# A new instruction order, engine choice and buffer slots for a fused adaLN attention and gMLP kernel

## The chip, the cores and the metric

The kernel runs on one core of one Trainium2 chip. The metric is device time in microseconds of one execution, as the median of several runs; smaller is better. The core has five instruction queues that run side by side and wait for each other by semaphores: PE (TensorE, matrix products), ACT (ScalarE), DVE (VectorE), POOL (GpSimd) and SP, which here only issues DMAs.

## The reference

Two blocks on x of 2048 rows and 448 columns in bf16, each behind a layernorm with a scale and a shift that come from a condition vector c:

```python
mod = (_silu(c) @ w_mod).reshape(1, 6, 1, -1)          # sa, ca, ga, sb, cb, gb
h = _layernorm(x) * (1 + ca) + sa
x = x + ga * _A_ref(h, A_wqkv, A_wo)                   # 16 heads of 28, causal, window of 256 keys
h = _layernorm(x) * (1 + cb) + sb
x = x + gb * _B_ref(h, B_w_in, B_w_sp, B_b_sp, B_w_out)
# _B_ref:
z = _gelu(x @ w_in); z1 = z[..., :896]; z2 = _layernorm(z[..., 896:])
g = w_sp @ z2 + b_sp[:, None]                          # mixes the 2048 positions
return (z1 * g) @ w_out
```

## The kernel before

All data stay in SBUF. The 2048 rows are 16 tiles of 128 (j or t below) or 4 blocks of 512 (tb). The program first makes a list of 1236 numbered operations, each with the engines that it may run on, its dependencies, and the buffers that it takes from pools of slots. The order in which they are issued, on all engines at once, is a string of words, `ORDER`. A word is number, engine (p, a, v, g, s for PE, ACT, DVE, POOL, SP) and the slot of each buffer taken:

```python
for word in ORDER.split():
    n, eng, *slots = word.split(".")
    op, e = self.ops[int(n)], ENGS["pavgs".index(eng)]
    ...
    for h, k in zip(op.take, slots):
        h.slot = h.res.options[int(k)]
    ...
    self.prog[e].append(op)
```

Each engine's program is the words of that engine in their order. Waits on semaphores are then worked out from dependencies and slots (an operation that takes a slot waits for all users of its former owner), so every order is a correct program as long as it doesn't deadlock. Durations in the list (`dur`) no longer decide anything. 42 warming products of the list stand in neither string.

The stages, with the lines that the profile shows and the numbers of operations that matter here:

- *Start.* SP loads x (0, 1 the first two halves of 224 KB; 14, 17, 18 the rest), parts of w_mod (3, 4, 5), and the weights of q (6, 7, 8), k (9, 10, 11) and v (12, 13). Line 561 are products that only keep PE busy. Line 596/597 pads the q and k weights (130 to 137), lines 605 to 627 normalise x, line 692 transposes on PE, line 699/701 scales the result into hT (163 to 173), line 740 is the first q and k product (174 on), line 767/768 evicts it.
- *Attention, for j from 0 to 15, two halves each.* Line 952 is the wide score block (434 is the first of this kind, 819 the last), line 961 a further block of scores; line 913 on ACT is the exponential: one of 128 x 2048 (PW, 1.88 us) and one of 128 x 512 for each half, 128 x 1024 for the first two j (383 is the first). Line 968 on DVE masks, line 995 on PE multiplies with V, lines 1009 and 1011 divide into one of three o_sb slots. A DMA transpose on SP puts that into hT (line 477, hT<-o_sb), line 1019 multiplies with wo (801 for j = 14, 830 for j = 15), line 1024 adds to x, lines 605 to 633 normalise again, a second DMA transpose (hT<-xn) follows, and line 1044 scales it on ACT, DVE or POOL. Products of later blocks (line 782 q and k, 824 v, 811 the last k) are strewn between these, with the evictions of lines 792, 816 and 828. The four wide score banks are one buffer, so each wide score block waits for the exponential before it.
- *gMLP in.* Line 1081 makes z (gelu 1092/1104 on ACT; normalised by lines 605 to 617 and 1096/1099, or by 1108 to 1118), line 1127 makes z1 (gelu 1135).
- *Mixing.* 28 groups (line 1151) of 16 products of 128 x 512: each needs all 16 tiles of z and all 16 slices of one half of w_sp, wspA (863 + 1 + slice: operations 864 to 879) for tb 0 and 1, or wspB (880 to 895) for tb 2 and 3. These slices are DMA transposes of SP too. wspA lies where the attention's q buffers were: six of its slices may be loaded before the attention ends, the others and all of wspB not. Line 1155 on DVE adds the bias (bsp_bc, loaded by 863 with one plain DMA of 512 KB), line 1158 on POOL multiplies with z1.
- *Out.* Line 1170 multiplies with w_out, seven products for a tile, line 1181 on DVE adds x, line 1186 stores. The last tile is cut into three column pieces (1224/1225, 1228/1229, 1232/1233 on PE; 1226, 1230, 1234 on DVE; 1227, 1231, 1235 on SP).

## Time and profile before

| | |
|---|---|
| median of 3 runs | 274.05 us (273.52 to 274.32) |
| span of the profiled execution, first to last instruction | 271.3 us |
| PE busy | 262.8 us, 97% of the span |
| DVE, ACT, POOL busy | 154.9, 137.9, 105.6 us |
| PE weight loads busy (beside PE) | 142.2 us |
| HBM read and written | 9.53 and 1.84 MB |

The time of the profiled execution itself is not recorded beside its span; the runs' median is 2.75 us above the span. "Busy" counts an engine while at least one of its instructions runs; instructions that only wait, branch or issue a DMA don't count. A name such as `ps<-wspA,z` is output<-inputs; PEld is PE's loading of weights, which runs beside its products; SPq is SP's issuing.

### The profile page before, as it was taken

To read this page: it belongs to the slowest core of one execution; us is meant where nothing else is said; L and a number is where in the kernel's file an instruction comes from. 1 tells how busy PE (TensorE), PEld (TensorE's weight loads), DVE (VectorE), ACT (ScalarE), POOL (GpSimd) and SP (SyncE) were. 2 spreads that over 40 slices of the span, in tenths; PEclk is the share of its full clock that TensorE was granted. 3 is DMA by queue.
4 is the path that set the end of the run, shared out by engine and by line. 5 is a ranking of instruction groups with operands and counts; after the bars stand their busy time and mean duration, and the time that the engine had idled before them with its cause. 6 is when DMAs were issued, how large, how long until landed. Compare 5 with 4: busy or idle time off the path is not lost.

```text
span 271.3 us, 7454 instructions
## 1 busy us (share of the span) xinstructions
PE 262.8 (97%) x3207; PEld 142.2 (52%) x3231; DVE 154.9 (57%) x380; ACT 137.9 (51%) x190; POOL 105.6 (39%) x161
## 2 busy tenths in 40 slices
PE   6899999999999999999999999999999999999995
PEld 3665565666578665444544444444444444444543
DVE  6789996999999999998382001131102230136623
ACT  3699999999999997799996400000000000000000
POOL 8740528101244533671558401565003631155220
PEclk9999999999999999999999999999999999999999
DMA  7959846442137678557999999600000000001212
GB/s 212 305 195 339 140 109 90 81 61 41 21 65 128 86 98 158 106 111 105 162 205 175 184 211 167 78 0 0 0 2 0 0 0 2 0 0 49 86 53 85
DMA packets 67594, 26.53 MB, mean 98 GB/s; under 512 B 58021, under 2 KB 66474, under 8 KB 67562
## 3 DMA queue, kind: packets, MB, share of 16 engines
q1 hardware_dynamic: 67288, 25.61, 47.8%
q8 instruction: 25, 0.41, 0.7%
q10 hardware_dynamic: 274, 0.46, 0.4%
q14 instruction: 7, 0.06, 0.1%
HBM read 9.53 MB, written 1.84 MB: 42 GB/s over the span
## 4 chain that ended last, share of the span: by engine, by line
PE 84%; ACT 9%; DVE 2%; DMA 2%; issue 2%; SPq 1%; DVEq 0%
PE ps L1151 35%; PE ps L1081 8%; PE ps L1127 8%; PE ps L1170 8%; PE ps L782 5%; ACT PW L913 5%; PE ps L995 5%; PE ps L952 4%; PE ps L1019 4%; PE ps L824 3%; PE ps L961 2%; DMA wq_st<-in_A_wqkv_dram 2%; DVE hT L728 1%; PE ps L811 1%; ACT qT L767 1%
## 5 line engine op out<-in xcount | busy, mean ns | idle before, releaser
L913 ACT ACTIVATE PW<-ps 128x2048 bf16<-128x2048 f32 (+1 forms) x56 | 67.9, 1255 | 1.8 <-PE ps L952 0.7
L1155 DVE TENSOR_TENSOR tmpg<-ps,bsp_bc 128x512 bf16<-128x512 f32 x28 | 19.0, 689 | 85.6 <-PE ps L1151 74.0
L1158 POOL TENSOR_TENSOR z1T<-tmpg,z1T 128x512 bf16<-128x512 bf16 x28 | 31.9, 1152 | 75.3 <-DVE tmpg L1155 75.3
L1151 PE MATMUL ps<-wspB,z 128*128 128x512 bf16 x218 | 48.8, 379 | 0.3
L1151 PE MATMUL ps<-wspA,z 128*128 128x512 bf16 x219 | 48.6, 379 | 0.4 <-POOL z L1096 0.2
L968 DVE TENSOR_TENSOR PT<-PW,mask 128x1024 bf16<-128x1024 bf16 x56 | 36.7, 683 | 0.7 <-ACT PW L913 0.7
L1151 PEld LDWEIGHTS ps<-wspA,z 128*128 128x128 bf16 x224 | 21.9, 98 | 26.7 <-POOL z L1096 0.5
L1151 PEld LDWEIGHTS ps<-wspB,z 128*128 128x128 bf16 x224 | 21.9, 98 | 26.3
L613 POOL TENSOR_TENSOR rs_all<-ve_all,neghalf 128x1 f32<-128x1 f32 (+1 forms) x31 | 20.6, 674 | 33.7 <-DVE ve_all L610 32.4
L995 PE MATMUL ps<-Vaug,PT 128*128 128x32 bf16 x496 | 23.9, 177 | 0.0
L995 PEld LDWEIGHTS ps<-Vaug,PT 128*128 128x128 bf16 x496 | 21.9, 96 | 3.8 <-DVE o_sb L1011 0.6
L1170 PE MATMUL ps<-w_out_g,z1T 128*128 128x448 bf16 (+2 forms) x126 | 21.9, 332 | 0.0
L1081 PE MATMUL ps<-w_in,hT 64*128 64x448 bf16 x224 | 21.9, 349 | 0.0
L1127 PE MATMUL ps<-hT,w_in 64*128 64x512 bf16 x196 | 21.8, 376 | 0.0
L995 PE MATMUL ps<-Vaug,PW 128*128 128x32 bf16 x224 | 20.1, 176 | 0.0
L605 DVE BATCH_NORM_STATS2 st_all<-x_sb 128x6 f32<-128x448 bf16 x32 | 19.0, 611 | 0.0
L995 PEld LDWEIGHTS ps<-Vaug,PW 128*128 128x128 bf16 x224 | 17.6, 96 | 2.2
L782 PE MATMUL ps<-hT,WQK 128*128 128x512 bf16 x67 | 17.3, 379 | 1.3 <-DVE PT L988 0.2
L1170 PEld LDWEIGHTS ps<-w_out_g,z1T 128*128 128x128 bf16 x126 | 11.7, 98 | 10.0
L1135 ACT ACTIVATE z1T<-ps 128x512 bf16<-128x512 f32 x28 | 14.3, 609 | 4.2 <-PE ps L1127 4.2
L1081 PEld LDWEIGHTS ps<-w_in,hT 64*128 64x128 bf16 x224 | 10.7, 94 | 10.6 <-ACT PW L913 0.4
L952 PE MATMUL ps<-qT,KT 32*128 32x64 bf16 (+2 forms) x1008 | 15.3, 198 | 0.3 <-ACT PW L913 0.2
(122 smaller groups left out, 339.6 us busy)
## 6 DMA issues: line engine op xcount, KB each, us to landing
out_dram<-fin SPq DMA_DIRECT2D x15, 112.0 KB, 1.7
x_sb<-in_A_x_dram SPq DMA_DIRECT2D x3, 448.0 KB, 5.3
wmod<-in_w_mod_dram SPq DMA_DIRECT2D x1, 1344.0 KB, 9.5
w_in<-in_B_w_in_dram SPq DMA_DIRECT2D x1, 1344.0 KB, 9.1
QBD<-qT SPq DMA_DIRECT2D x16, 64.0 KB, 2.4
w_out_g<-in_B_w_out_dram SPq DMA_DIRECT2D x1, 784.0 KB, 6.6
bsp_bc<-in_B_b_sp_dram SPq DMA_DIRECT2D x1, 512.0 KB, 5.9
x_sb<-in_A_x_dram SPq DMA_DIRECT2D x2, 224.0 KB, 3.5
```

The costliest lines, as they stand in the source:

```text
L605: st = [dve(0.62 if True else 0, lambda e, t=t, ci=ci, s=s: e.bn_stats(st_all[:, slot, t, ci, :], s()), deps(t), prio) for ci, s in enumer ...
L613: rs = pool(0.41 + 0.155 * len(tiles), lambda e: e.tensor_tensor(rs_all[:, slot, a:b], ve_all[:, slot, a:b], neghalf[:, 0:b - a], ALU.pow) ...
L782: m = pe(4 * MMS, [lambda e, h=h, g=g, kc=kc, tb=tb: e.matmul(ps[:, h.slot[0], :], lhsT=WQK[:, kc, 4 * g:4 * g + 4, :].rearrange("p a b -> ...
L913: ex = act(xdur, lambda e, out_ap=out_ap, in_ap=in_ap: e.activation(out_ap(), in_ap(), ACT.Exp, scale=SCALE), [s], v - 8.0 + u, takes, tab ...
L952: fm.append(lambda e, hm=hm, k=k, qi=qi, key=key, kn=kn, lo=lo, hi=hi, col=col, p0=p0, t=t, j=j: e.matmul(ps[p0:p0 + kn, hm.slot[t], k * 1 ...
L968: return dve(0.68, lambda e: e.tensor_tensor(cols(hp.slot[0] * 2048 + 1024 * k, [[256, 4], [128, 2], [1, 128]]), cols(at_w() + 128 + 192 * ...
L995: fns.append(lambda e, hp=hp, hO=hO, hi=hi, bi=bi, kb=kb, hd=hd, nb=nb, a=at[hi][bi], p_of=p_of: e.matmul(ps[:, hO.slot[0], 32 * hd:32 * h ...
L1081: return lambda e, kc, p0, start, stop: e.matmul(ps[:, hs[t % 2].slot[hf], 0:D], lhsT=hT[p0:p0 + 64, kc, t * 128:(t + 1) * 128], rhs=w_in[ ...
L1127: return lambda e, kc, p0, start, stop: e.matmul(ps[:, hs[b // 2].slot[b % 2], :], lhsT=w_in[p0:p0 + 64, kc, ft * 128:(ft + 1) * 128], rhs ...
L1151: m = pe(16 * MMS, [lambda e, h=h, si=si, ft=ft, tb=tb: e.matmul(ps[:, h.slot[0], :], lhsT=z2[:, si, ft * 128:(ft + 1) * 128], rhs=(wspA i ...
L1158: u = pool(1.16, lambda e, ht=ht, ft=ft, tb=tb: e.tensor_tensor(z1T[tb][:, ft, :], tmpg[:, ht.slot[0], :], z1T[tb][:, ft, :], ALU.mult), [ ...
L1170: return [lambda e, ft=ft: e.matmul(ps[:, h.slot[0], c0:c1], lhsT=z1T[t // 4][:, ft, (t % 4) * 128:(t % 4 + 1) * 128], rhs=w_out_g[:, ft, ...
```

## The change

Only the string `ORDER` is replaced. It comes from a newly written search that uses distances measured in the trace of the kernel before. The same 1194 numbered operations are issued. Their order on every engine is new; 108 of the operations that may go to two or three engines change engine (37 from DVE to POOL, 30 from POOL to DVE, 20 from ACT to DVE, 17 from DVE to ACT, 2 each way between ACT and POOL); and most buffer slots are others. The lines that matter here, from both strings:

```diff
-2.a 25.v 35.g 0.s 26.v 27.v 28.v 38.g 39.g 3.a 4.s 36.g 45.a 33.g 29.v 5.s 30.v 31.v 37.g 32.v 40.g 6.s 7.s 41.g 46.p.0 48.a 47.a 144.v 8.s 145.v 1.s
...
-266.a 434.p.0 285.v 252.a 117.s 269.p.1 282.v 279.v 435.a.4.0 115.s 286.v 419.v 387.p 391.p 280.v 393.p 284.v 263.p.0 227.v 287.v 336.v 270.a 288.g
...
-985.p.1 808.v.0 923.g 809.v 943.a 901.v 986.p 810.s 987.p 944.v 903.v 988.a 937.v 966.p.0 873.s 924.v 945.a.0 967.p.3 936.v 955.v 968.p 995.a 874.s
...
-845.g 1110.p.6 1059.a 883.s 840.g 1058.a 1057.a 1088.a 893.s 1089.a 1056.a 1140.p.7 894.s 886.s 887.s 1107.p.0 891.s 863.s 892.s 1104.p.1 884.s 895.s
-1134.p.2 889.s 885.s 1131.p.3 1135.v.0 1105.v.1 1136.g 1098.p.4 1132.v.0 1133.g 844.g 1106.g 1095.p.5 1137.p.2 1096.v.0 1108.v.1 1097.g 841.g 1141.v.0
...
-1212.p.1 1187.s 1222.v.3 1223.s 1213.p 1224.p.4 1214.v.2 1225.p 1228.p.2 1229.p 1232.p.3 1226.v.0 1215.s 1233.p 1227.s 1234.v.1 1235.s 1230.v.3 1231.s
+0.s 3.a 35.g 25.v 28.v 36.g 38.g 2.a 4.s 37.g 33.g 61.p.3 26.v 5.s 34.g 65.p.5 42.g 1.s 72.p.5 57.p.1 43.g 7.s 45.a 58.p.5 39.g 138.v 8.s 46.p.1
...
+245.p.1 250.v 219.s 385.p.0 416.a 387.p 246.v 220.s 113.p.0 247.v 23.s 227.a 434.p.0 282.v 390.v 114.a 280.v 251.p.1 285.v 435.a.0.0 115.s 283.v 118.s
...
+856.v 932.p.1 833.v 779.v.0 834.g 857.v 1043.a 835.g 933.p 780.v 855.v 781.s 858.a 902.v 836.g 934.p 808.g.2 935.a 955.v 984.p.0 903.v 809.g 904.v
+1042.a 954.v 837.g.1 810.s 985.p.3 943.a 838.g 986.p 905.g 839.s 966.p.2 988.a 967.p.1 989.v 868.s 987.p 956.v 990.v 968.p 995.a 870.s 969.p 860.g
...
+863.s 1030.a 873.s 963.g 1003.p 999.g 1004.p 844.g 1005.a 1076.p.2 945.a.0 846.g 1006.v 1077.p.0 1025.v 869.s 1013.a 1078.p 1026.v 946.v 1007.v
...
+1086.p 977.g 887.s 1087.p 842.g 1095.p.4 1091.a 895.s 1088.a 1089.a 1059.a 893.s 1090.a 1058.a 884.s 1104.p.0 883.s 882.s 1107.p.1 880.s 890.s 889.s
+1134.p.2 888.s 894.s 1098.p.3 1135.v.0 886.s 1136.g 1125.p.2 1099.v.0 1206.p.3 1137.p.5 1207.v.1 1208.g 840.g 1108.v.1 1109.g 1158.p.6 1161.p.1
...
+1179.p.0 1183.v.1 1184.s 1188.p.1 1180.v.0 1181.s 1224.p.0 1189.v.2 1225.p 1228.p.2 1190.s 1226.v.3 1229.p 1232.p.1 1230.v.1 1227.s 1233.p 1231.s
+1234.v.0 1235.s
```

The order of SP behind the attention, in words: before, wspA slices 864 and 865 were issued among the hT transposes, then the other 14 of wspA, 11 of wspB, the bias load 863, and 5 of wspB. After, 872, 865, 866 and 876 are issued among the hT transposes; behind the last of these come 6 of wspA, the bias load, 3 of wspA, 2 of wspB, 3 of wspA, and 14 of wspB. The mixing groups ran in the order tb 0, 1, 0, 0, 1, 1, 0, 0, 1, 1, 2 (1170), 2, 3 and so on; now they run tb 0, 0, 0, 1, 0, 1, 3 (1206), 1, 2 and on.

More of the change, by code (lines that the diff above doesn't have):

```diff
@@ new lines @@
+594.p 646.a.3.4 540.p.0 400.v 513.v 401.v 456.v 639.p.0 595.v 514.v 355.p.1 613.v 515.g 428.g 402.g 596.v.0 640.a 666.p.0 429.g 541.v 614.p.0
+667.a.4.1 620.v 618.p.0 615.p 359.p.0 457.v 621.v 458.g 430.g 622.p 459.v 619.a 360.v 460.g.0 674.p.0 356.v 647.p.0 675.a.1.2 431.g.1 623.p 353.p.0
+624.v 403.g 461.v 432.v 516.g 625.v.1 462.s 326.p.1 354.v 648.a 678.v 695.p.0 327.a 597.s 357.p.0 641.v 696.a.2.3 642.v 668.p.0 626.s 643.p.0 671.v
+365.p.1 679.v 358.a 124.s 669.a 703.p.0 649.v 366.a 121.s 644.p 699.v 676.p.0 704.a.5.0 367.p.0 361.s 650.v 362.s 569.p.1 670.v 364.s 651.p 404.g.2
```

92 lines of the change are left out of this document (43 added, 49 removed).

## The prediction

> **What bounds the kernel now.** I read the page first (busy shares, then the chain of waits), then the windows by stage, and then the single places that the change touches. The page:
>
> ```profile
> span 271.3 us, 7454 instructions
> PE 262.8 (97%) x3207; PEld 142.2 (52%) x3231; DVE 154.9 (57%) x380; ACT 137.9 (51%) x190; POOL 105.6 (39%) x161
> ...
> PE 84%; ACT 9%; DVE 2%; DMA 2%; issue 2%; SPq 1%; DVEq 0%
> ```
>
> PE is busy for 262.8 of 271.3 us and makes up 84% of the chain. The windows (start:end, length, then the busy time of each engine) show where the missing 8.5 us are:
>
> ```profile
> 0.00:10.00 10.00, 7.37 (x67) 3.93 (x68) 6.99 (x25) 4.60 (x9) 7.04 (x20) 1.00 0.85 248
> 10.00:30.00 20.00, 18.92 (x268) 12.04 (x269) 17.95 (x56) 18.53 (x32) 8.24 (x14) 1.00 0.87 263
> 30.00:105.00 75.00, 73.87 (x1854) 49.15 (x1863) 69.94 (x153) 73.25 (x77) 27.78 (x42) 1.00 0.50 77
> 105.00:150.00 45.00, 45.00 (x464) 21.57 (x458) 31.60 (x103) 38.48 (x69) 25.45 (x54) 1.00 0.84 153
> 150.00:260.00 110.00, 109.25 (x510) 50.63 (x518) 23.79 (x37) 3.04 (x6) 35.97 (x33) 1.00 0.27 49
> ```
>
> PE idles 2.63 us before 10 us (it has nothing landed), 1.08 us from 10 to 30, 1.13 us in the attention (30 to 105), nothing from 105 to 150, and 0.75 us from 150 to 260; the rest is the end. In the attention ACT (73.25 of 75) and DVE (69.94 of 75) are almost as full as PE. The change leaves every matmul in place, so a better order can win only these idle times. What lies between 10 and 260 us is 1.08 + 1.13 + 0.75 = 2.96 us; with the end (below) some 3.3 us is the most that can be had. Nothing limits a loss in that way. Durations below are of this profiled execution, whose span is 271.3 us; the median of the runs, 274.05 us, is 2.75 us longer, and I carry that difference over unchanged. Differences under 0.3% (0.82 us) are about what a measurement of this kernel can't tell from none.
>
> **The start.** In the new order SP issues the second x half (1) ahead of the q weights (7, 8, 6), and on DVE and ACT the operations of the first tiles are dealt out anew.
>
> ```profile
> 3.05 4.63 DMA wq_st<-in_A_wqkv_dram
> 8.68 2.98 PE L740 MATMUL ps<-hT,WQK 128*128 128x256 bf16 x23 [0.43 <-DVE hT L701]
> ...
> x_sb<-in_A_x_dram SPq DMA_DIRECT2D x2, 224.0 KB, 3.5
> wq_st<-in_A_wqkv_dram SPq DMA_DIRECT2D x2, 224.0 KB, 4.5
> ```
>
> The q weights land at 3.05 + 4.63 = 7.68 us and the first product runs at 8.68. With 224 KB of x ahead of them instead of 112 KB of weights they land some 0.45 us later (half of 224 KB at the 248 GB/s of the first window). But before, the DVE did one of the weight paddings and then two hT evictions one after the other; now ACT evicts the first hT chunk while DVE pads. That gives 0.4 us back. I take 0 for the first product, with ends of +0.5 and -0.4.
>
> **The attention.** From the list of the new order: fewer products stand ahead of the first wide score block (434). Gone from before it are 265 and 251, four products of line 782 each.
>
> ```profile
> 46.03 1.76 PE ps L782 x8
> ...
> 26.35 1.88 ACT L913 ACTIVATE PW<-ps 128x2048 bf16<-128x2048 f32 x1
> ...
> 102.24 3.01 ACT L913 ACTIVATE PW<-ps 128x512 bf16<-128x512 f32 x3
> ...
> L913 ACT ACTIVATE PW<-ps 128x2048 bf16<-128x2048 f32 x28 | 53.0, 1894 | 1.5 <-PE ps L952 0.7
> L913 ACT ACTIVATE PW<-ps 128x512 bf16<-128x512 f32 x28 | 17.3, 617 | 0.3
> ```
>
> Eight products are 1.76 us, so PE reaches that block about 1.7 us of work sooner. Whether the attention also ends sooner is ACT's matter: from the first wide exponential at 26.35 to the end of the last at 105.25 ACT works through 28 wide ones of 1.89 us, with smaller operations of about 0.6 us between them. I counted these between the first and the last wide one: 51 before, 49 after, thus 1.2 us less of ACT work. On the other hand six operations that stood behind the first score exponential now stand ahead of the first wide one (19 from 383 to 435 against 13). So the first wide one starts only 0 to 1 us sooner, and the last ends between 0 and 2 us sooner if nothing else waits. In the attention alone PE can give 1.13 us. I take an attention that ends 0.3 us sooner, near the lower end, because PE, ACT and DVE are all over 93% busy there.
>
> **The weights of the mixing stage: what is late next.** After the attention SP has one row of transposing loads to issue, and PE starts the mixing stage (line 1151) when all 16 slices of wspA have landed and all z are ready.
>
> ```profile
> 118.58 6.34 SPq L477 DMA_TRANSPOSE hT<-xn  x4
> 124.96 19.74 SPq L477 DMA_TRANSPOSE wspA<-in_B_w_sp_dram  x14
> 144.74 15.89 SPq L477 DMA_TRANSPOSE wspB<-in_B_w_sp_dram  x11
> 160.68 0.58 SPq L1056 DMA_DIRECT2D bsp_bc<-in_B_b_sp_dram  x1
> 161.30 9.35 SPq L477 DMA_TRANSPOSE wspB<-in_B_w_sp_dram  x5
> ...
> 150.33 1.62 PEld L1151 LDWEIGHTS ps<-wspA,z 128*128 128x128 bf16 x9 [0.49 <-POOL z L1096]
> ...
> 150.56 10.74 PE ps L1151 x49
> 161.35 10.74 PE ps L1151 x49
> ...
> L1096 POOL TENSOR_SCALAR z<-z,rs_all,ve_all 128x896 bf16<-128x896 bf16 x4 | 4.3, 1087 | 0.7 <-DVE ve_all L617 0.7
> ...
> DMA to landing us min/median/max: 3.0/4.0/5.0
> ...
> DMA to landing us min/median/max: 3.5/4.1/6.4
> ```
>
> (The two landing lines are those of wspA and of wspB.) A transpose takes 19.74 / 14 = 1.41 us of the queue. The 5 behind the bias load take 9.35, so that load costs 0.6 + 9.35 - 5 x 1.41 = 2.9 us of queue. The new order issues four wspA slices early, where the old one issued two, and moves the bias load (863) from behind 11 wspB slices to behind 6 wspA slices. The last wspA slice is again the 14th of the final row, now with the bias ahead of it: it is issued at 124.96 + 13 x 1.41 + 2.9 = 146.2 and lands 3.0 to 5.0 later, at 149.2 to 151.2, 150.2 by the median. Before, the stage started at 150.33, 0.49 us late for a z on POOL; in the old order four such z of 1.09 us stood in one block at POOL's end, in the new one two of them come earlier, so the last z is up to 2.2 us sooner. So the transfers take the place of the z wait: a start at 150.2, unless the row of transposes starts earlier too. Even a faster PE before it would wait here.
>
> The new order also runs a group on wspB (1206) as the seventh, where the first was the eleventh. One group is 16 products; the pieces of the chain step by 10.79 us for 50 (49 recorded), so 3.45 us each, and the seventh starts at 150.3 + 20.7 = 171.0. The last wspB slice was issued at 161.30 + 9.35 - 1.41 = 169.2; with two fewer in the row it goes at 166.4 and lands 3.5 to 6.4 later, 170.5 by the median. The wait for it is 0 by the median, at most 1.8 us. I take 0.1. The other transfers that were moved (the x and w_in loads in the attention) land many microseconds ahead of use.
>
> **The end.** Of the last tile's three column pieces DVE now evicts 1230 before 1234, in the order in which PE makes them; before, it waited for the last piece first.
>
> ```profile
> 268.19 1.38 SPq L1186 DMA_DIRECT2D out_dram<-fin  x3
> 268.46 0.46 DVE L1181 TENSOR_TENSOR fin<-ps,x_sb 128x112 bf16<-128x112 f32 x2 [0.30 <-PE ps L1170]
> ...
> 236.84 1.32 PE ps L1170 x7
> ...
> L1181 DVE TENSOR_TENSOR fin<-ps,x_sb 128x448 bf16<-128x448 f32 (+2 forms) x18 | 10.0, 570 | 9.0 <-PE ps L1170 8.3 <-DMA out_dram<-fin 0.6
> ```
>
> Both small evictions came after PE's end (0.46 us), and the last of three issues ended at 268.19 + 1.38 = 269.57. With one eviction and one issue under PE's last products, one issue fewer stands at the end: 1.38 / 3 = 0.46 at most, 0.37 taken. The other late groups use three PSUM banks in turn, but one eviction (0.57 us) fits under each 1.32 us of products, so I cost that at nothing; if that cover fails, it is some 0.6 us once.
>
> **Sum of the forecast:** start 0, attention -0.3 (which reaches the end only as far as the transfers let it: -0.1), wait for wspB +0.1, end -0.4: span 270.9, time **273.7 us**. Its own range is 273.2 to 274.9, mostly within 0.3%.
>
> **Rivals.**
>
> *The lead goes through (faster).* If ACT turns its shorter row and the earlier first block into an attention that ends 1.2 us sooner, the last hT transposes (118.58 to 124.92) and the row behind them move too, and with the end 0.4 us that is 274.05 - 1.6 = **272.4 us**. For it: 1.2 us less of ACT work and less idle PE from 10 to 30. Against: the last hT are now scaled on POOL (808, 809, 837, 838), one after the other.
>
> *The bias load pushes the weights (slower).* If it blocks the queue as badly as at 161.30 or worse and a landing takes the maximum, wspA lands at 151.2 and wspB at 172.8 against a need at 171.0: PE loses 1.8 us in all. From a landing after 171.0 on each microsecond counts in full. 274.05 - 0.4 + 1.8 = **275.5 us**.
>
> *POOL and DVE get in each other's way in the attention (slower).* The change moves more operations to POOL (39 to it, 30 off it), among them hT and xn scalings.
>
> ```profile
> L1044 POOL TENSOR_SCALAR hT<-hT,modT x2: 767/1200/1632, 91.8 to 101.0; 128x512 bf16<-128x512 bf16 x2
> ```
>
> The same scaling on POOL took 767 ns once and 1632 ns once. Twelve of these long ones are new on POOL and ten are gone. If three of the twelve stretch by 0.87 us and hold up DVE and with it PE, that is 2.6 us: 274.05 - 0.4 + 2.6 = **276.3 us**. Against: DVE's work in the attention stays the same, and POOL is under 40% busy there. [...]
>
> That the new order does nothing but its better end (273.7) is in the forecast.
>
> **How the numbers follow.** Forecast 0.35; the lead goes through 0.31; the bias load 0.2; POOL and DVE 0.1; something slower that I don't see (a buffer slot that is wanted again too early, o_sb among them, whose slots no longer go round in turn) 0.04. Faster by over 0.3% (under 273.23) is the second case and a little of the forecast: 0.33. Slower by over 0.3% (over 274.87) is the last three: 0.34 with a little of the forecast put in: 0.35. Within: 0.32. For 8 in 10 the range goes from 271.9 (the lead and 0.5 us at the start) to 276.4 (the POOL case).
>
> **What would show it.** Right: the first load of weights of line 1151 waits for a DMA and not for POOL, at about 150; the seventh group starts near 171; the last issue to out_dram ends near 269.0 in an otherwise equal span; idle PE from 30 to 105 stays near 1.1 us. The lead: the last wide exponential ends before 104.3 and wspA's row from before 124. The bias: a gap of PE of over 0.5 us at the seventh group. POOL: line 1044 or 684 on POOL with a mean over 1.2 us. The prediction would be wrong if PE idles much more than 1.1 us in the attention or if PE's busy time itself changes.

## The result: slower by 2.5%, and the time is lost ahead of the mixing stage

| | before | after |
|---|---|---|
| median of the runs beside each other | 274.19 us (273.52 to 274.82) | 280.74 us (280.25 to 281.16) |
| ratio, 95% interval | | 1.0251 (1.0223 to 1.0278) |
| profiled execution: time, span | span 271.3 us | 280.85 us, span 278.9 us |

The forecast was 273.7 us, the range up to 276.4. In a second comparison the same new order took 281.21 us, 1.0295 of before (1.0264 to 1.0325): its times spread more than those of before (280.25 to 283.59), for a reason that the profiles below show. A ratio leaves out executions that took over 1.5% more than the fastest of the same kernel (two of six in e1, one of five in e9, two of six in e14, one of six in e15, four of seven in e17; their mean clock was 0.988 or 0.994), while a median counts every execution.

The two profiled spans are 7.6 us apart, the medians 6.55. The profiled execution of before was one of its shortest: later executions of it with the same span of 271.3 us took 273.0 to 273.1 us, about 1 us less than the median of 274.05 that the prediction set beside this span.

All lines of the profile of after stand one higher than before (L952 is L953). The page of after: 3.0 us more of busy PE (part of it products at half clock in the first 12 us, below), and a chain of waits of which PE makes up 70%, before 84%:

```profile
span 278.9 us, 7451 instructions
PE 265.8 (95%) x3209; PEld 142.3 (51%) x3231; DVE 158.3 (57%) x376; ACT 137.3 (49%) x187; POOL 111.5 (40%) x168
...
PE 70%; DVE 12%; issue 6%; POOL 5%; ACT 3%; DMA 3%; DVEq 0%; POOLq 0%
```

The same windows as in the prediction (PE's busy time is the third number): 7.04, 18.52, 71.52 and 43.70 against 7.37, 18.92, 73.87 and 45.00. PE idles 3.5 us in the attention, where before it idled 1.13, and 1.3 us from 105 to 150, where it idled not at all.

```profile
0.00:10.00 10.00, 7.04 (x56) 3.51 (x57) 6.12 (x22) 4.47 (x8) 5.61 (x18) 1.00 0.85 244
10.00:30.00 20.00, 18.52 (x250) 12.27 (x250) 18.69 (x52) 17.51 (x30) 6.56 (x11) 1.00 0.49 153
30.00:105.00 75.00, 71.52 (x1786) 46.30 (x1789) 69.36 (x153) 70.16 (x74) 30.88 (x44) 1.00 0.56 102
105.00:150.00 45.00, 43.70 (x500) 21.48 (x500) 30.75 (x91) 36.81 (x62) 28.02 (x56) 1.00 0.87 150
```

PE's waits in after (line, what it waited for, us in total, times, longest) show new places. Three are waits for c (line 519), for hT of block 2 (line 783), and "issue", which is no wait for any engine. The first row is a wait for a DVE copy: it names line 618, the last DVE instruction to end, but the product reads WQK, which DVE's copy 137 had been writing until just before (rows below).

```profile
PE ps L741 <- DVE ve_all L618: 1.2, 1, 1.2
PE ps L519 <- DMA c_row<-in_c_dram: 1.1, 1, 1.1
PE ps L783 <- DVE mv_all L609: 1.1, 2, 0.9
PE ps L953 <- issue: 0.8, 1, 0.8
...
PE ps L1152 <- POOL z L1097: 0.7, 1, 0.7
...
PE ps L1020 <- DMA hT<-o_sb: 0.4, 1, 0.4
```

To add such places up I compared when PE starts a product with the work of the products ahead of it (each at its own rate at full clock). A wait of PE that the text gives without a row is counted in this way too, from one start to the next less the work of the product between; the idle time in a profile row, which counts from the end that the profile gives, is some 0.15 to 0.2 us less. The table gives how much later than in the order before PE is, in us, when it has done 2, 5, 30, 70, 75, 100 and 140 us of work (in after that is at 12.9, 18, 45, 87, 94, 122 and 165 us; 140 lies in the mixing stage). All rows are of the profiled executions.

| kernel | 2 | 5 | 30 | 70 | 75 | 100 | 140 |
|---|---|---|---|---|---|---|---|
| after | 2.30 | 3.40 | 4.05 | 5.08 | 6.46 | 7.26 | 7.77 |
| after again (e12) | 1.95 | 4.11 | 5.11 | 6.14 | 9.91 | 9.82 | 10.29 |
| e1 old start to 26 us | 0.35 | 0.35 | 2.18 | 3.30 | 3.22 | 3.96 | 4.29 |
| e2 c first | -0.29 | 0.93 | 0.79 | 1.82 | 2.96 | 4.97 | 5.25 |
| e3 pad on POOL | 1.79 | 3.73 | 4.88 | 5.91 | 9.48 | 9.42 | 10.03 |
| e4 before, w_mod first | 3.10 | 3.12 | 3.14 | 3.14 | 3.16 | 3.16 | 2.94 |
| e5 w_in early | 2.77 | 3.55 | 3.43 | 4.66 | 4.59 | 6.51 | 6.90 |
| e6 memsets away | 2.34 | 2.02 | 3.19 | 4.36 | 6.32 | 7.00 | 7.31 |
| e8 two slices late | 2.35 | 3.73 | 4.23 | 5.27 | 8.32 | 7.95 | 8.48 |
| e9 four places undone | 1.23 | 0.91 | 1.67 | 2.71 | 2.63 | 4.16 | 4.66 |
| e11 w_out behind | 2.85 | 3.50 | 3.40 | 4.44 | 7.00 | 7.52 | 9.17 |
| e13 old start to 174 | 1.50 | 1.25 | 1.14 | 2.17 | 5.97 | 5.52 | 6.56 |
| e15 and SP's order | 1.18 | 0.96 | 1.62 | 2.79 | 2.71 | 2.20 | 3.03 |

The 7.77 us of after fall into 2.3 at the start, 1.1 more by 5 us of work, 0.65 to 30, 1.0 to 70, 1.4 between 70 and 75, 0.8 to 100, 0.5 to the mixing stage. Behind that hardly anything changes any more (the spans are 7.6 us apart). The 1.0 us between 30 and 70 stands in every row with the new attention, and no run took it away; it goes in small pieces, of which 0.3 us is PE's longest wait there.

### The profile page after: what moved, and what is told of

Read it like the earlier page. It is cut to its first block, busy times and chain, and to the rows that moved or that the text cites. A ratio compares the mean times of both kernels' runs of the same rounds, so it can differ in the third digit from the quotient of the medians.

```text
span 278.9 us, 7451 instructions
## 1 busy us (share of the span) xinstructions
PE 265.8 (95%) x3209; PEld 142.3 (51%) x3231; DVE 158.3 (57%) x376; ACT 137.3 (49%) x187; POOL 111.5 (40%) x168
## 3 DMA queue, kind: packets, MB, share of 16 engines
HBM read 9.53 MB, written 1.84 MB: 41 GB/s over the span
## 4 chain that ended last, share of the span: by engine, by line
PE 70%; DVE 12%; issue 6%; POOL 5%; ACT 3%; DMA 3%; DVEq 0%; POOLq 0%
PE ps L1152 34%; PE ps L1171 8%; PE ps L1082 7%; DVE PT L969 3%; PE ps L996 3%; PE ps L953 2%; PE ps L741 2%; PE ps L1020 2%; PE ps L825 2%; ACT PW L914 2%; PE ps L1128 2%; PE ps L783 2%; DVE st_all L606 2%; POOL rs_all L614 2%; DMA hT<-o_sb 1%
## 5 line engine op out<-in xcount | busy, mean ns | idle before, releaser
L614 POOL TENSOR_TENSOR rs_all<-ve_all,neghalf 128x1 f32<-128x1 f32 (+1 forms) x31 | 20.2, 657 | 18.9 <-DVE ve_all L611 16.8
L1182 DVE TENSOR_TENSOR fin<-ps,x_sb 128x448 bf16<-128x448 f32 (+2 forms) x18 | 10.1, 571 | 25.3 <-PE ps L1171 25.0
L996 PE MATMUL ps<-Vaug,PW 128*128 128x32 bf16 x224 | 20.2, 176 | 0.0
L611 POOL TENSOR_SCALAR ve_all<-mv_all 128x1 f32<-128x1 f32 (+1 forms) x16 | 4.3, 272 | 37.2 <-DVE mv_all L609 33.4
L1136 ACT ACTIVATE z1T<-ps 128x512 bf16<-128x512 f32 x28 | 15.0, 602 | 3.1 <-PE ps L1128 3.0
```

The source lines that it names most:

```text
L614: rs = pool(0.41 + 0.155 * len(tiles), lambda e: e.tensor_tensor(rs_all[:, slot, a:b], ve_all[:, slot, a:b], neghalf[:, 0:b - a], ALU.pow) ...
L996: fns.append(lambda e, hp=hp, hO=hO, hi=hi, bi=bi, kb=kb, hd=hd, nb=nb, a=at[hi][bi], p_of=p_of: e.matmul(ps[:, hO.slot[0], 32 * hd:32 * h ...
```

## The experiments

What stands ahead of each "Measured" was written before the run; theory A and the rival are its forecasts. Beside these runs the order before had medians of 273.23 to 273.56 us.

### The start: which load comes first

On ACT the old order issues c and then 448 KB of w_mod, the new one the other way round. Timeline of before:

```profile
0.79 0.51 ACTq L422 DMA_DIRECT2D c_row<-in_c_dram  x1
...
2.07 0.37 PE L518 MATMUL ps<-one,c_row 1*128 1x1 bf16 x4 [2.07 <-DMA c_row<-in_c_dram]
...
2.38 3.94 PE L561 MATMUL ps<-ident 128*128 128x512 bf16 x9
...
3.60 0.63 DVE L605 BATCH_NORM_STATS2 st_all<-x_sb 128x6 f32<-128x448 bf16 x1
...
8.68 2.55 PE L740 MATMUL ps<-hT,WQK 128*128 128x256 bf16 x19 [0.43 <-DVE hT L701]
```

and of after:

```profile
0.79 0.48 ACTq L414 DMA_DIRECT2D wmod<-in_w_mod_dram  x1
1.31 0.60 ACTq L423 DMA_DIRECT2D c_row<-in_c_dram  x1
...
4.52 0.63 DVE L606 BATCH_NORM_STATS2 st_all<-x_sb 128x6 f32<-128x448 bf16 x1 [1.97 <-DMA x_sb<-in_A_x_dram]
...
5.20 0.37 PE L519 MATMUL ps<-one,c_row 1*128 1x1 bf16 x4 [1.11 <-DMA c_row<-in_c_dram]
...
10.43 2.44 PE L741 MATMUL ps<-hT,WQK 128*128 128x256 bf16 x13
```

c's product runs at 5.20 instead of 2.07, x's statistics start at 4.52 instead of 3.60, and the first q and k product runs at 10.43 instead of 8.68. In 2.44 us it gets 13 products done, where before 19 took 2.55: the clock is still at half, up to 12.17 (ahead of that the products of this row start 0.21 us apart, behind it 0.11). (The windows show 1.00 here, because the trace's clock record begins only with the rise, at 6.11 us before and 12.17 after.)

**e2: c first again.**

```diff
-0.s 3.a 35.g 25.v 28.v 36.g 38.g 2.a 4.s
+0.s 2.a 3.a 35.g 25.v 28.v 36.g 38.g 4.s
```

> The new order with one word moved: ACT issues the load of c (2) ahead of the 448 KB of w_mod (3), as it did before. Theory A (the swap sets the start: c lands late, x behind it, PE idles 1.1 us among its warming products and its clock rises 6 us later): x lands near 3.5 instead of 4.50, PE idles no longer from 4.1 to 5.2, the first q and k product runs at 9.0 to 9.4 instead of 10.43, at full clock; 1.2 to 2.0 us less, thus 278.7 to 279.5 us. Rival (other operations set the start: a memset (27) queued behind the first statistics of x on DVE, w_mod's middle part landing at 6.59): 280.3 to 281, and the first product within 0.4 us of 10.43.

Measured: the profiled execution took 278.44 us against 280.85, its first q and k product ran at 8.54 at full clock, and at 2 us of work it was 2.59 us ahead of after. So theory A holds for the start of this execution. Over 1 us of that lead is the clock, which was up by 7 us here: e9 (below) has the same first words and products, its clock rose at 11.03, and at 2 us of work it leads after by 1.07 us. The five other executions of e2 took 280.05 to 282.59 us; the median is 280.50, in the rival's range, and the ratio is 1.0255 (1.0220 to 1.0291), as in after. Their mean clock was 0.988 or 0.994 where the profiled one had 1.0. So what was won at the start was lost again, as far as the mean clock tells, to half clock, of which more below.

**e4: the swap alone, in the order before.**

```diff
-2.a 25.v 35.g 0.s 26.v 27.v 28.v 38.g 39.g 3.a 4.s
+3.a 2.a 25.v 35.g 0.s 26.v 27.v 28.v 38.g 39.g 4.s
```

> The order before with one word moved: ACT issues the 448 KB of w_mod (3) ahead of the load of c (2), as the new order does; nothing else differs from before. Theory A (this swap alone costs at the start): the product that turns c (line 518) runs at 4.5 to 5.5 instead of 2.07, PE has no work from 0.8 to then, its clock rises later, and the first q and k product runs 1 to 2 us later: 275.2 to 276.2 us. Rival (in the old order enough stands around it to hide the late c): 274.0 to 274.5 us.

Measured: 275.99 us, ratio 1.0097 (1.0072 to 1.0122); c's product at 5.22, the first q and k product at 11.93. PE is 3.1 us late at 2 us of work and 2.9 at 140 (table). This is theory A: the time is in its range, the start even later than it said. In the order before, where nothing else differs, this one word costs 2.6 us; in the new order, putting it back moved the median by nothing that the runs can tell (e2).

**e13: the whole old start**, 74 words up to the first q and k product, then the rest of the new order.

> The order before up to the first q and k product (174, its first 74 words), and behind it everything that is left in the new order. Theory A (the start is lost by the order of the first loads and by warming products that no longer run as one row, which keeps the clock at half to 11 to 13 us): the first q and k product runs at 8.5 to 9.3 us, at full clock by 7 us, 2.1 to 2.5 us less than the new order at that point; the DVE copies beside POOL's memsets and the w_in load stay as they are, so 277.5 to 279.5 us with a spread of over 1 us. Rival (later waits take it back, as in the run with the load of c put back by itself): 280 to 281 us.

Measured: 279.05 us, 1.0202 (1.0178 to 1.0226); first product at 9.02, clock up at 6.20. The time is theory A's. The point at 2 us of work is only 0.8 us better than after, because at the seam between the two strings ACT's memset 50 now stood ahead of the eviction 164 (PE waited 1.46 us).

**e1: the old order up to 26 us**, then the new one.

> The order before up to the first wide score block (434, near 26 us), and behind it everything that is left in the new order, with the engines and slots of the string that each word comes from. In the new kernel product work that stands at 26.4 us in the old one stands at 29.3 (2.9 us late), and 4.9 us more are lost behind that, at single places up to the mixing stage. Theory A (the losses add up, each at its own place): the 2.9 us come back and the 4.9 stay: 277.9 us. Theory B (the later stalls come of the late start, as x blocks and their transposes were planned for an earlier front): most of them go too: 274 to 275.5 us. Theory C (the end is set by ACT and DVE in the attention, and a lead of PE at the front is lost there): 280 to 281 us.

Measured: 278.08 us, 1.0157 (1.0138 to 1.0177), which is theory A's; two of the six executions took 282.05 and 282.78. Of the loss at the start 0.35 us is left, but at the second wide score block PE waits 1.76 us (1.58 in the row) for the first wide exponential, which starts at 26.80 (before: 26.35). So the first wide block, 1.7 us of PE work sooner, brings no lead: ACT with its six extra operations is no earlier than it was.

### DVE beside POOL

Timeline of after, DVE's pad 137 and what POOL does beside it:

```profile
12.58 1.22 POOL L505 MEMSET Vaug<- 128x256 bf16 x1
...
13.24 2.42 DVE L597 COPY WQK<-wq_st 128x448 bf16<-128x448 bf16 x1
13.38 2.15 POOL L532 MEMSET QBD<- 128x1024 f32 x2
```

**e3: the pad on POOL, ahead of the memsets** (`137.v` becomes `137.g` ahead of `41.g`).

> The new order with one word moved: the last weight pad (137) goes to POOL, ahead of a Vaug memset, instead of to DVE, where it took 2.42 us beside three POOL memsets and PE waited 1.38 us for it. Theory A (DVE's copy was locked out while the memsets ran, and PE's wait is real loss): 137 takes about 0.56 us and ends near 13.2, product 195 follows 193 without a wait, 1.0 to 1.4 us less: 279.4 to 279.8 us. Rival (what PE gains there it loses at the next wait, for the transposes of x tiles 2 and 3, whose xn 155 came at 16.16): 280.3 to 280.8 us. If the lock stands, one of the DVE operations that now run beside the memsets takes over a microsecond.

Measured: 281.42 us, 1.0306 (1.0271 to 1.0341). The pad takes 0.55 us on POOL, but another operation of DVE, a scaling that reads and writes SBUF, is hit in its place, and worse:

```profile
13.18 1.23 POOL L505 MEMSET Vaug<- 128x256 bf16 x1
13.29 2.98 DVE L626 TENSOR_SCALAR xn<-x_sb,mv_all,rs_all 128x448 bf16<-128x448 bf16 x1
13.99 2.15 POOL L532 MEMSET QBD<- 128x1024 f32 x2
```

PE waits 2.06 us for it. Both theories on the time fail; that a DVE operation takes over a microsecond beside the memsets holds. Here as in after it ends 0.13 us after the last of the three (16.27 and 16.14 here, 15.66 and 15.53 in after).

**e6: the memsets away** (`41.g` ahead of `140.g`, `49` and `52` on ACT).

> The new order with three memsets taken away from beside the DVE copies of the start: 41 stays on POOL but ahead of 140 (near 3.3 us), 49 and 52 go to ACT, behind 135 and 184. Theory A (in the run with the pad on POOL the scaling 155 took 2.98 us in place of the pad's 2.42, and both ended 0.1 us after the last memset: DVE's copies are locked out as long as POOL's memsets follow each other): 137 takes about 0.27 us and 155 about 0.4 us, neither PE wait remains (1.4 us at 15.72), and 1.0 to 1.6 us come back: 279.0 to 279.7 us. Rival (it is DVE's own queue, or a wait that the profile puts elsewhere): 137 or 155 still take over 1.5 us, 280.3 to 280.8 us.

Measured: the pad 0.27 us and the scaling 0.40, no wait of PE at either (timeline of e6), 1.4 us better than after at 5 us of work: theory A for the two operations. The time is the rival's, 280.42 us, 1.0244 (1.0204 to 1.0284): the gain doesn't reach the end, and again five of six executions had a mean clock of 0.993 or 0.994.

```profile
13.29 0.27 DVE L597 COPY WQK<-wq_st 128x448 bf16<-128x448 bf16 x1
...
13.66 0.40 DVE L626 TENSOR_SCALAR xn<-x_sb,mv_all,rs_all 128x448 bf16<-128x448 bf16 x1
```

**e18: the same pad on DVE in the order before** (`137.g` becomes `137.v` ahead of `169.v`).

> The order before with one word changed: the pad 137 runs on DVE, ahead of 169, and not on POOL, so that a DVE copy which takes about 0.27 us alone meets POOL's memsets 49, 51 and 52, which then run back to back from about 11.6 us. Theory A (a DVE copy is locked out as long as POOL's memsets follow each other, whatever the order around it): 137 takes 1 to 3 us and ends within 0.2 us of the end of one of the memsets; PE waits for it ahead of product 194, 0.5 to 2.5 us longer: 273.9 to 275.9 us. Rival (the long copy belongs to the new order alone): 137 takes under 0.5 us, 273.0 to 273.6 us.

Measured: 274.04 us, 1.0024 (1.0009 to 1.0039), in theory A's range. Not the pad (0.35 us, as the rival said) but the scaling 161 ahead of it met POOL's memsets: the mask's was running when it started, the first of QBD had moved up behind that, and the scaling took 1.22 us (0.40 before) and ended 0.13 us after the second of them; PE waited 1.29 us for it (0.43 before):

```profile
11.34 0.31 POOL L506 MEMSET mask<- 128x256 bf16 x1
11.45 1.22 DVE L625 TENSOR_SCALAR xn<-x_sb,mv_all,rs_all 128x448 bf16<-128x448 bf16 x1
11.59 0.95 POOL L531 MEMSET QBD<- 128x1024 f32 x1
```

So the long DVE operation beside memsets is no property of the new order. The old one had others beside its three memsets of QBD (0.95 us each, between 12.22 and 15.20 us), and these took there what they take on the mean of the run: three evictions of hT from PSUM 0.40 to 0.41 us (mean 0.406), four statistics of x 0.59 to 0.62 (mean 0.611). In the long cases DVE's operation ended only behind the last of two memsets in a row (e18) or of three (after, e3).

### The w_in load and PE's stop without a wait

The new order issues 1344 KB of w_in at 86.83 us (before: 20.79). Five us later PE stops in the middle of a score block, whose products wait for nothing any more. SP's and PE's rows in after:

```profile
86.83 0.59 SPq L403 DMA_DIRECT2D w_in<-in_B_w_in_dram  x1
...
92.92 0.18 PE L953 MATMUL ps<-qT,KT 32*64 32x64 bf16 x1 [0.78 <-issue]
```

**e12: the new order once more.**

> The new order itself once more, for comparison within one call. 1.023 to 1.028 of the order before. Theory A on PE's stop at 92 us (it hangs on when a block of instructions comes through the DMA queues past the w_in load): the stop is there again, with another length between 0.3 and 3 us, and the time spreads by 2 us or more from run to run. Rival (a fixed cost of the order): the stop is 0.7 to 0.9 us again and the times lie within 0.5 us.

Measured: 281.21 us (280.25 to 283.59). The stop is there again, 2.31 us long (its row), and behind it the granted clock falls to half, likewise behind the 2.07 us that PE waited at the pad (windows; the clock is the third number from the right):

```profile
95.67 0.18 PE L953 MATMUL ps<-qT,KT 32*64 32x64 bf16 x1 [2.31 <-issue]
```

```profile
16.00:18.00 2.00, 1.85 (x23) 1.14 (x24) 1.96 (x8) 0.44 (x1) 0.00 (x0) 0.98 0.98 290
18.00:20.00 2.00, 2.00 (x7) 0.71 (x5) 1.97 (x7) 1.50 (x3) 0.00 (x0) 0.50 0.09 19
...
96.00:98.00 2.00, 2.00 (x30) 1.88 (x27) 0.00 (x0) 1.97 (x2) 0.00 (x0) 0.61 1.79 185
98.00:100.00 2.00, 2.00 (x76) 1.67 (x74) 1.85 (x4) 0.85 (x2) 0.00 (x0) 0.54 0.94 103
```

The DMA records point at what PE waited for. One queue moves blocks of 16 KB marked as instructions (25 of them, 0.41 MB, on the page of before and on that of after); in the profiles without such a load in the attention one starts every 3.5 to 6.5 us from 70 to 100 us. In the eight profiles that have w_in in the attention and the new order around it, one block comes 7.5 to 9.3 us after the one ahead of it, and PE goes on 1.3 to 1.6 us after the end of that block each time: 91.38 and 92.92 (after), 93.81 and 95.41 (e3), 91.32 and 92.72 (e6), 94.22 and 95.67 (e12). The stop was 0.78, 0.51, 2.93, 1.79, 2.31, 2.08, 2.31 and 2.22 us long (idle time in its row) in after, e2, e3, e6, e8, e11, e12 and e13. In e5, e9, e14, e15 and e17, which load w_in at the start, there is no such stop. That PE waited there for its own program behind the big load is the author's estimate from these times; the records don't show whose instructions a block holds.

**e5: w_in behind the loads of the start** (`21.s` right behind `16.s`).

> The new order with one word moved: the 1344 KB load of w_in (21), which the new order issues at 86.83 us ahead of the transposes 406 and 684 (the order before: 20.79 us), goes behind the last loads of the start, near 10.5 us, where the DMA engines then stand idle from 18 to 24 us. Theory A (behind this load the transposes land up to 6 us late, and PE's own instructions too: PE stopped for 0.78 us at 92.14 in the middle of a score block with no wait on any engine): the stop at 92 is gone, 684 lands within 3 us of its issue instead of 4.5, and one or more of the waits for transposes at 105.61 (0.56), 112.28 (0.29) and 121.04 (0.91 us) shrink; 1.0 to 3.0 us less: 277.7 to 279.7 us. Rival (ACT and DVE set the pace there; PE stops at the next exponential instead): 280 to 280.8 us.

Measured: 279.55 us, 1.0193 (1.0153 to 1.0232), all six executions at full clock, no stop, and between 70 and 75 us of work nothing is lost (after: 1.4). The transpose 406, which stood right behind the load, lands 3.07 us after its issue instead of 7.19; 684 takes 3.94 instead of 4.47, where theory A said under 3. The time is theory A's. Part of the gain goes again at the last o_sb transpose, for which PE now waits 1.84 us instead of 0.91.

**e7: w_in late, in the order before** (`21.s` behind `363.s`).

> The order before with one word moved: the 1344 KB load of w_in (21) goes from 20.79 us to behind the last q transfer (363, near 79.5 us), ahead of the transposes 491, 626 and 655. Theory A: PE stops within 6 us behind it with nothing to wait for that the profile shows (issue), for 0.5 to 3 us, and transposes land 3 us or more later; 0.7 to 3 us longer: 274.2 to 276.5 us on a chip where the order before takes 273.4. Rival (such a load in the attention is harmless in itself): within 0.4 us of the order before.

Measured: 274.10 us, 1.0023 (0.9998 to 1.0047). PE loses 0.65 us between 75 and 100 us of work, but doesn't stop; the block of instructions behind the load comes 6.6 us after the one ahead of it. The time lies between the two theories and is hardly to be told from no change. So this load, put there, didn't stop PE; that it hangs on when the next block of instructions is due is the author's estimate and not shown.

### Half clock

Seven of the profiles hold half-clock stretches behind the first rise, nine in all (mean clocks of these profiles: 0.987 to 0.994). Each lasted 3.41 us (one of them twice that) and began a whole number of periods of 3.413 us after the clock's first rise: 2 and 25 of them in e3 and in e12, 24 in e6 and e11, 25 in e13, 14 in e17, 13 in e14. (In before and after the record has full clock for 266.24 us from the first rise, 78 such periods.) What goes with them is PE's idle time within one such period (its length less PE's busy time in that window). In the period that ended where half clock began it was 1.64 to 2.47 us in all nine cases. In no other period behind the first rise and ahead of 260 us was it over 1.61 us (e10; 1.08 in after), in any profile that has the record of the clock. As the ends of products are modelled, the border between is not exact. A stop that lay across two periods had no half clock behind it: that of 2.31 us in e8, whose mean clock was 1.0, put 1.39 into the one period. Why one stretch, in e14, lasted two periods is not shown. One stretch costs, by an estimate from the granted 0.5, half its length, 1.7 us: the 0.006 by which the mean clock of the longer executions is low.

The first rise belongs here too. It came at 5.2 to 8.1 us in the ten profiles that start in the old way, at 11.0 to 13.2 in eight of the nine that start in the new way (PE begins at 1.8 to 2.3 us in all of them); the ninth, e2, had it by 7 us (its warming product at 6.31 took 0.38 us, where those of after up to 10 us took 0.59 to 0.64), with the same products in the same order as e9, so part of this is chance. The old start runs nine warming products in one row ahead of the 32 small products of w_mod; the new one strews these between them. No run here changed that order alone, so why the rise comes late stays open.

### Undoing several places

**e9: four places at once** (c first; memsets away; w_in early; `475.v` ahead of `476.v`).

> The new order with four places put back, six words in all: the load of c (2) ahead of w_mod (3) on ACT; the memsets 41 (earlier on POOL), 49 and 52 (on ACT) away from DVE's copies; the w_in load (21) near 10 us instead of 86.83; the mask 475 on DVE ahead of 476, as PE wants it first. Theory A (each place is a loss of its own, about 2.4, 1.4, 1.6 and 0.45 us by the runs before this): they add up, 5.9 us less than the new order: 274.3 to 275.5 us on a chip where the order before takes 273.4. Rival (some of what PE gains early it waits for later, at ACT's exponentials or at the transposes from 100 us on): 276 to 278 us.

Measured: 277.35 us, 1.0133 (1.0113 to 1.0154), in the rival's range. About 1.2 us of what is missing is a clock that rose at 11.03, with the same row of products that in e2 ran fast at 7 us. And from 75 to 100 us of work it loses 1.5 us, at the transposes, as the rival said.

**e8: two wspA slices out of the attention** (`872.s` and `865.s` behind `868.s`, `892.s` and `891.s` behind `879.s`).

> The new order with the wspA slices 872 and 865, which SP issues at 91.87 and 95.33 between the transposes of the attention (1.2 to 2.2 us of queue each), moved into the final row behind 868, and two wspB slices (892, 891) moved behind the last of wspA so that wspA lands when it did. Theory A (each slice pushes the transposes behind it, on which wo's products wait): the transposes 713 and 771 go some 2 to 4 us earlier, the waits at 105.61 (0.56 us) and 112.28 (0.29 us) go: 0.5 to 1.0 us less, 279.7 to 280.2 us. Rival (SP has slack there, the transposes wait for their o_sb and not for the queue): 280.5 to 281 us.

Measured: 280.23 us, 1.0240 (1.0199 to 1.0280). The waits at 714, 772 and 830 are gone, but PE had stopped 2.31 us at 92, so the transposes had time anyhow: inconclusive.

**e11: the w_out load behind the last o_sb transpose** (`381.s` behind `829.s`).

> The new order with one word moved: the 784 KB load of w_out (381), issued at 112.72 ahead of the transposes 800 and 829 (which landed 7.05 and 5.25 us after their issue), goes behind 829. Theory A (a large plain load holds up the transposes behind it, here the last two that wo's products wait for): 829 lands within 3 us of its issue, PE's wait for it at 121.04 (0.91 us) goes, and 0.4 to 0.9 us come back: 279.8 to 280.4 us. Rival (the transposes 636 to 694, now behind the load, come late in turn): PE waits as long for them near 125 us, 280.5 to 281.2 us.

Measured: 282.24 us, 1.0329 (1.0308 to 1.0349), above both ranges; all four executions had a mean clock of 0.994, as with one half-clock stretch. 829's wait went, and instead PE waited 1.23 us at 128 us for a gelu of z (960), which stood on ACT behind an operation that waited for POOL (927, its input at 126.08): from 100 to 140 us of work it loses 1.65 us, in after 0.51. That is the rival's kind of loss, at another place than it said; that the moved load is behind POOL's lateness there isn't shown.

**e14: the old start to 174, with memsets, w_in and 475 put back.**

> As the run before (the old start up to the first q and k product), with three further places put back: memsets 49 and 52 on ACT, the w_in load (21) behind the loads of the start, the mask 475 ahead of 476. Theory A (the run with four places undone lost 1.2 us to a clock that rose at 11.03 us; all of it goes): 275.8 to 276.6 us where the order before takes 273.4, no stop without a wait near 90 us, and no half clock behind 8 us in any run. Rival (what comes early at the start waits at ACT's first exponentials): 277 to 278 us.

**e15: and SP's order** (433 and 655 ahead of 684, slices 872 and 865 and two of wspB late).

> As the run before, with SP's order changed too: the transposes 433 and 655, whose inputs are ready 10 to 20 us earlier, go ahead of 684, which waits for its o_sb; the wspA slices 872 and 865 go into the final row, and two wspB slices behind the last of wspA. Theory A (in the new order the transposes that PE waits for at 714, 772 and 830 are late because the queue is full by its own order): the waits at 714 (0.77 us) and 772 (0.52 us) go or halve, 829 stays late behind the w_out load; 0.6 to 1.3 us less than the run before: 275.0 to 275.8 us. Rival (PE then waits elsewhere, for DVE or ACT, whose order is the new one): the same as the run before within 0.3 us.

Measured: e14 took 277.78 us, 1.0154 (1.0133 to 1.0176), in the rival's range; e15 took 276.97, 1.0128 (1.0096 to 1.0160), 0.8 us less. From 75 to 100 us of work e15 loses nothing against before, where e9, with the same attention but SP's new order, loses 1.5 us; PE's waits for the transposes are gone from its list. That is theory A by the profile, though its time (275.0 to 275.8) wasn't reached; the times alone, with overlapping intervals, wouldn't show it. In SP's new order, 684 waits for its o_sb while 433 and 655, ready 13 and 4 us earlier, stand behind it; 713 then is issued 3.7 us after its o_sb in e9, 0.6 in the order before.

**e17: and `50.a` behind `164.a`.**

> As the run with SP's order changed, with one more word moved: on ACT the QBD memset 50 goes behind the hT eviction 164, which it held up by 1.46 us ahead of the second q and k product (that order came of the seam between the old start and the new rest). Theory A (each named place is a loss of its own): the wait of 1.46 us goes, 0.8 to 1.5 us less than the run before: 275.0 to 276.2 us where the order before takes 273.3, and the places named so far make up some 5 to 6 of the new order's 7.5 us. Rival (PE waits longer for ACT's exponential 383 and its successors): within 0.3 us of the run before.

Measured: the executions fall in two groups, 275.88 to 276.85 (1.0095, 1.0059 to 1.0130) and 280.19 to 281.29. The first group's ratio is 0.9 us below that of e15, as theory A said, but the intervals overlap, and its median of 276.59 us is above theory A's range. At 2 us of work the profiled execution is 0.10 us late, where e15 is 1.18: the wait at the seam is gone. The profiled one is of the second group, and shows DVE and POOL slow each other once more (timeline): four masks of 0.68 us take 1.45 each, in step with POOL's products on wo_g, of which the first had started first (46.56 against 46.68) and the others take 1.49 instead of 1.04; PE then waits 3.17 us, and half clock follows. (e14's profile shows the same, its executions fall apart likewise: 277.2 to 277.9, and 282.0 and 284.0.)

```profile
46.56 5.39 POOL L590 TENSOR_TENSOR wo_g<-wo_g,gg_sb 128x448 bf16<-128x448 bf16 x4 [3.07 <-DMA gg_sb<-mod_rows]
...
46.68 5.81 DVE L969 TENSOR_TENSOR PT<-PW,mask 128x1024 bf16<-128x1024 bf16 x4
```

In after it is the other way round: DVE was first (47.84 against 48.17), its masks take 0.69, and POOL's first product took 3.67 us (groups: before, then after).

```profile
L589 POOL TENSOR_TENSOR wo_g<-wo_g,gg_sb 128x448 bf16<-128x448 bf16 x4 | 4.0, 1036 | 0.0
```

```profile
L590 POOL TENSOR_TENSOR wo_g<-wo_g,gg_sb 128x448 bf16<-128x448 bf16 x4 | 7.2, 1830 | 2.9 <-DMA gg_sb<-mod_rows 2.9
```

With these places put back, the new order thus comes from 1.0251 and 1.0295 to 1.0095 of before in three of seven executions; in the other four it takes 280.19 to 281.29 us, as much as the new order itself. The profiled one of these four lost its time beside the products on wo_g and in the half clock behind them. The last 2.6 us of the faster group (0.0095 of 273.56) were not taken apart; the 1.0 us between 30 and 70 us of work is among them.

### The mixing stage and the end

**e10: the old order up to 137 us, then the new one.**

> The order before up to its word 1076 (near 137 us, the z1 stage), and behind it everything that is left in the new order: the bias load ahead of the last wspA slices, the new order of the mixing groups with one on wspB as the seventh, and the new end. Theory A (the prediction's own step: the new mixing and end by themselves give 0.2 to 0.5 us): the last product to the end of the span takes 2.5 us instead of 2.86, PE starts the mixing stage at 150.1 to 150.8, no gap at the seventh group: 272.8 to 273.3 us where the order before takes 273.4. Rival (the transfers behind the bias load come too late): a start of the mixing stage after 151.3 or a gap of over 0.5 us at the seventh group, 273.9 to 275.5 us.

Measured: 277.65 us, 1.0149 (1.0127 to 1.0171): the mixing stage starts late, as the rival said, and the time is above its range. But the seam makes two waits of its own (1.5 and 1.6 us for gelus on ACT), and with only two wspA slices issued early, where the new order has four, the last one landed at 154.81, which is when the stage starts. So it shows that with the bias load and two wspB slices ahead of the last of wspA there is no slack left (it landed at 147.43 before), and nothing on the new stage by itself.

**e16: the new end alone** (`1230.v` and `1231.s` ahead of `1234.v`).

> The order before with the new end alone: DVE evicts 1230 ahead of 1234, and SP stores 1231 ahead of 1235. The prediction's own step said 0.37 us less, 0.46 at most: 272.9 to 273.1 us where the order before takes 273.4. The traces of the two orders say less: from the last product's end to the end of the last issue it is 1.14 us before and 1.10 after, since one small eviction and one store stand behind the last product in both: 273.2 to 273.4 us.

Measured: 273.30 us, 1.0006 (0.9984 to 1.0028). From the last product's end to the end of the last issue it takes 1.10 us, as in after, against 1.14 before.

## Why the prediction was wrong, step by step

- **What can be won.** Right: at most 3.3 us, and no bound on a loss. The chances didn't follow from that sentence; two thirds stood on faster or no change.
- **The start, 0 with ends of +0.5 and -0.4.** This step failed: the first product was 1.75 us late, and PE was 2.3 us late with the clock. It looked at SP's loads of x and q weights, and q's weights did land about as said (8.10 to 8.60, said 8.1). But the two lists of words shown ahead of it begin with the swap of 2 and 3 on ACT, a load queue it never read, and it took the warming products for filling. In e4 the swap alone takes 2.6 us; in the new order itself e2 and e9 show about 1.1 us for it at the start, and over 1 us more that goes with the clock's rise.
- **POOL and DVE, a rival of 2.6 us at a chance of 0.1 and nothing in the forecast's sum.** That the two slow each other was right, the place wrong: not POOL's scalings of hT in the attention (lines 1045 and 685 have means of 0.865 and 0.810 us, under the sign of 1.2), but memsets at the start (1.4 us at 5 us of work, e6) and wo_g. The term was sized by three stretches of 0.87 us; one DVE scaling took 2.98 us instead of 0.40, beside three POOL memsets in a row (e3). The rival has POOL's operation stretch and DVE wait with it. Both lost where they alternated, at the products on wo_g in e17 (POOL's 1.49 us instead of 1.04, DVE's masks 1.45 instead of 0.68); beside the memsets it was DVE that lost, and POOL's memsets of QBD took 1.05 us on the mean in after, 0.95 before. (32 operations left POOL, not 30.)
- **"The other transfers that were moved ... land many microseconds ahead of use."** True of w_in itself (first used at 109.9), and beside the point: what stands behind it in the queues came late, transposes (406 landed 7.19 us after its issue, in e5 3.07) and, by the author's estimate, PE's program. That cost 1.4 us between 70 and 75 us of work (e5), and up to 3.8 with half clock (e12). SP's order of the other transposes cost 1.5 us more (e9 against e15).
- **PE's clock.** The sum had no term for it. Its first rise came 6.06 us later in after than before, and each half-clock stretch behind a stop costs, by the estimate above, 1.7 us.
- **The attention ends 0.3 us sooner.** Failed: the last wide exponential ends at 108.99 (before 104.62). The first wide score block came 1.4 us later in time although 1.7 us of work sooner; e1 shows that even with the old start ACT doesn't begin sooner.
- **The transfers take the place of the z wait.** Half right: the last slice went about as long behind the start of SP's row as said, but z came later still. The last wspA slice went 20.2 us after the row's start (predicted 21.2) and landed 4.9 us later, at 157.25; but the last z was ready only at 158.05, and PE waited for POOL:

```profile
L1152 PE MATMUL ps<-wspA,z 128*128 128x512 bf16 x220 | 48.8, 379 | 0.8 <-POOL z L1097 0.7
```

- **The seventh group.** Right: it started 20.5 us after the stage (predicted 20.7), 2.95 us after the last wspB slice had landed; no wait.
- **The end, -0.37.** Failed: 0.04 us by the traces, no change in time (e16). The step took one issue of 0.46 off, but eviction and issue of the last piece stand behind the last product in either order.
- **The bias load as the bound (275.5).** It didn't decide; e10 shows how near it was.

## What to carry to other kernels

Where PE is 97% busy, read every queue's first words against the old ones: one moved word that put a large load ahead of a tiny one at the start cost 1% here (e4). A big transfer that was itself in time held up transposes here (406 landed 7.19 us after its issue, 3.07 with the load at the start, e5) and, by the author's estimate, an engine's instructions; a stop of PE of about 2 us was in most profiles paid with some 1.7 us more at half clock. A list of durations for a search should know which DVE operations take longer beside POOL's: a copy of 0.27 us (e6) took 2.42 beside three memsets (after). And a wait that is taken away at one place need not shorten the whole: in the profiles e2 and e6 won 1.4 us and more by 5 us of work, and their medians hardly moved.

## What the runs showed that was not expected

- PE stood still for 0.5 to 2.9 us with every input ready, until 1.3 to 1.6 us after the end of a late 16 KB block marked as instructions (after, e3, e6, e12).
- Half clock came in periods of 3.413 us counted from the first rise, each time behind a period in which PE was idle for 1.64 us or more, and never behind one with 1.61 us or less.
- A DVE scaling of 0.40 us took 2.98 us over three POOL memsets; DVE masks took 1.45 us instead of 0.68 when POOL's product came first, POOL's product 3.67 us instead of 1.04 when the mask did.
- The same order of products had its clock up by 7 us in one execution (e2) and at 11.03 in another (e9).
